# The looks at the weights' range placed in the idle stretches of ScalarE, with a third load buffer (HGRN2 attention followed by a multiplicative feed-forward block, one core)

## The chip, the cores and the metric

The kernel runs on one core of a Trainium2 chip. The metric is the device time of one execution in microseconds (us), the median over several runs.

## The reference

The input is a gated linear attention (4 batches, 8 heads, 768 steps, head size 48) whose output, joined over the heads to 3072 tokens of 384 numbers, goes through a feed-forward block with two parallel up projections that are multiplied.

```python
f = 1.0 / (1.0 + np.exp(-f_logit))
for t in range(S):
    state = f[:, :, t, :, None] * state + np.einsum('bhd,bhe->bhde', k[:, :, t], v[:, :, t])
    y[:, :, t] = np.einsum('bhd,bhde->bhe', q[:, :, t], state)
x = np.ascontiguousarray(y.transpose(0, 2, 1, 3)).reshape(B * S, H * D)
a = x @ w1          # 384 x 1024
b = x @ w2          # 384 x 1024
h = a * b @ w3      # 1024 x 1024
out = h @ w_out     # 1024 x 384
```

The q, k, v and f_logit arrays are float32. The four weight matrices are double precision in memory and are read as pairs of 32-bit words. The product of `w3` and `w_out` is formed once on the chip ("folding").

## The kernel before

**Two stages.** The attention goes through 24 chunks of 128 steps (`front`, `turning`, `rest`), in the first 260 us or so. The feed-forward block goes through six blocks of 512 tokens (`ffn(n)`), beside the attention as far as its inputs are there. Blocks 1 and 2 compute the up projections with seven products in the place of eight (`seven`, its matrix products are recorded at L959). Blocks 3 to 5 use a longer scheme of the same kind (`many`), whose products stand at L1114: each is two matmuls of 128x128 by 256 columns into one PSUM bank, `bank()`. The down projection is `down(i)`, at L863, two for each block, each with seven groups of four matmuls.

**What follows a product of `many`.** Several products are added up in one bank, one behind the other in a chain (`CHAINS`). Wherever a partial sum is needed by itself, ScalarE copies the bank into a temporary (`keep_`, L1135), and the next product of the chain may write the bank only after that copy. VectorE adds temporaries and banks (L1158), multiplies halves into the input of the down projection (L1170, L1177), and forms sums of inputs (L1081) and, for `down`, of `ab` (L1224). The end of `down` is at L1231 and L1244 on ScalarE (copies of banks), and at L1237, L1250, L1261, L1267 and L1275 on VectorE; its results leave by the stores at L1280.

**PSUM.** Beside four tiles of one bank each, named `f`, the two tiles `pa` and `py` of the attention have two banks each. Once the attention is done, their four halves join the pool "f", so that a product may go to either half of `pa` or `py`.

**The looks.** The fast path is right only if the weights lie in a certain range. `ranges()` reads the high word of every double again: 34 pieces of 128x1024 words, `load(i)` at L1513 by the DMA queue of SyncE, then two looks by ScalarE, `total(i)` at L1517 (sum of absolute values) and `count(i)` at L1521 (count of values over a bound), each with an accumulator. The pieces alternate between two buffers, the halves of the tile `A` (`both`). `verdict`, `judge`, `told`, `heard` and `decided` turn the sums into one number, `left`, over memory and back. It is read by all engines at L1272 behind the last down projection, and a branch follows it (L240).

**The order of the work** is written by a planner (`Plan`). Every piece of work is a task with an engine, a cost, tasks that it depends on and a priority. `order()` takes again and again the task that can start first on the planner's clock, and among equals the one with the lowest `prio`. The tasks are then emitted in this order, and each engine executes its own tasks in that order. A task may hold a slot of a pool: "f" is the PSUM banks and "t" the temporaries of `many` (11 of them, six beside the homes; numbers 4 and 5 lie in the tile `place`, columns 12864 to 13887). `temporary(i)` says where each lies.

In the kernel before, a look is a task like the others with a priority above all others in number (500 + i), so it is taken when ScalarE would else wait on the planner's clock. The planner knows PSUM by single banks. What the program waits for is worked out later, from the tiles that the instructions read and write.

Of the kernel before, what the change touches and what calls it, by code (L numbers as in the profile page):

```python
# [36 lines left out]
F32 = mybir.dt.float32  # L37
I32 = mybir.dt.int32
U32 = mybir.dt.uint32
# [16 lines left out]
TB = 512  # L56
# [14 lines left out]
WIDE = 2 * HP * C  # L71
LOOK = WIDE // 2
# [7 lines left out]
SURE_W = 2.0  # L80
# [5 lines left out]
HEAVY = 3  # L86
WITH_POOL = 0.6
LOOKS = 0.0
QLATE = 0.1
MANY = 3  # L90
W_LATE = 30
# [31 lines left out]
class Plan:  # L123
# [13 lines left out]

        self.pools[name] = [None] * n

    def add(self, eng, cost, emit, deps=(), prio=0.0, takes=(), frees=(), lag=0.2, slack=0.0, since=0.0, shared=False):  # L140


        t = {
            "eng": eng, "cost": cost, "emit": emit, "deps": [d for d in deps if d is not None], "prio": prio,
            "takes": list(takes), "frees": list(frees), "lag": lag, "slack": slack, "since": since, "shared": shared, "at": None, "end": None, "no": len(self.tasks),
        }
        self.tasks.append(t)
        return t

    def order(self):  # L150
        free, done, left = dict.fromkeys(("PE", "DVE", "ACT", "POOL", "SP"), BEGIN), [], list(self.tasks)
        enders, masking = {}, []
        for t in self.tasks:
            for f in t["frees"]:
                enders.setdefault(id(f), []).append(t)

        def after(t, ds):

            if any(d["end"] is None for d in ds):
                return None  # L160
            return max([0.0] + [d["end"] + (d["lag"] + t["slack"] if d["eng"] != t["eng"] else 0.0) for d in ds])

        def places(t, name):

            ends = [(after(t, enders[id(h)]) if h else 0.0, i) for i, h in enumerate(self.pools[name])]
            return [e for e in ends if e[0] is not None]

        def start(t):

            waits, at = list(t["deps"]), max(free.get(t["eng"], 0.0), t["since"])  # L170
            for name in t["takes"]:
                if name in self.pools:
                    ends = places(t, name)
                    if not ends:
                        return None
                    at = max(at, min(ends)[0])
                    continue
                n, taken = self.slots[name]
                if len(taken) >= n:
                    waits += enders[id(taken[-n])]  # L180
            ready = after(t, waits)
            if ready is None:
                return None
            at = max(at, ready)
            if t["shared"]:
                at += WITH_POOL * sum(max(0.0, min(at + t["cost"], b) - max(at, a)) for a, b in masking[-2:])
            return at

        def rank(t):

            return t["deps"][0]["end"] - 1e6 if t["eng"] == "DMA" else t["prio"]

        def slower(t, at):

            big = t["cost"] > 0.7
            return max([1.0] + [by[big] for a, b, by in CROWDED if a <= at < b]) if t["eng"] == "DMA" else 1.0

        while left:
            at, _, _, t = min(
                ((at, rank(t), t["no"], t) for t in left if (at := start(t)) is not None), key=lambda x: x[:3]  # L200
            )
            t["at"], t["end"] = at, at + t["cost"] * slower(t, at)
            free[t["eng"]] = t["end"]
            if t["eng"] == "POOL" and t["cost"] > 1.0:
                masking.append((t["at"], t["end"]))
            for name in t["takes"]:
                if name in self.pools:
                    t["got"] = min(places(t, name))[1]
                    self.pools[name][t["got"]] = t
                else:  # L210
                    self.slots[name][1].append(t)
            left.remove(t)
            done.append(t)
        return sorted(done, key=lambda t: (t["at"], t["no"]))
# [46 lines left out]
def ranged(ctx, tc, q, k, f_logit, v, w1, w2, w3, w_out, out, ident, w12, wc, left):  # L261
# [39 lines left out]
    def at(a, *shape):  # L301
        n = 1
        for m in shape:
            n *= m
        t = place[:, a : a + n]
        return t.rearrange("p (a b) -> p a b", a=shape[0]) if len(shape) == 2 else t
# [21 lines left out]
    def home(i):  # L328

        if i not in found:  # L330
            found[i] = homes[i]()
        return found[i]

    plan = Plan()
    plan.pool("f", NF)
    plan.pool("t", len(homes) - NWT + 6)
    plan.slot("a", 1)
    plan.slot("lane", 8)
    plan.slot("heavy", HEAVY)
# [13 lines left out]
    def temporary(i):  # L353

        if i < 2:
            return firsts[i]
        if i < 4:
            return ups[("u2", "u3")[i - 2]]
        return at(12864 + TB * (i - 4), TB) if i < 6 else home(NWT + i - 6)

    def idle(n):

# [67 lines left out]
    def moves(n, size, rate, emit, deps, prio, late=0.0, since=0.0, lanes=("lane",)):  # L430


        for j in range(n):
            i = plan.add("SP", 0.45, (lambda: None) if j else emit, [d] if j else deps, prio - j * 1e-3, takes=lanes, lag=0.85, since=since)
            d = i
            t = plan.add("DMA", size / n / rate, lambda: None, [i], prio - j * 1e-3, lag=1.1 + late, frees=[i])
        return t
# [1063 lines left out]
    def ranges():  # L1501

        seen = [w[kc * P : kc * P + P] for w in (w1, w2) for kc in range(KM)] + [w3[jc] for jc in range(KF)]
        seen.append(w_out.rearrange("(p a) c -> p (a c)", a=KF))
        seen = [w[:, c : c + LOOK] for w in seen for c in range(0, w.shape[1], LOOK)]
        n = len(seen)
        sums_, counts, small = (spare[:, a : a + m] for a, m in ((0, n), (64, n), (128, 1)))
        words = both.bitcast(U32)
        hi = words.rearrange("p (n two) -> p n two", two=2)[:, :, 1].bitcast(F32)
        last = [plan.add("DVE", 0.1, lambda: nc.vector.memset(small, -SMALL), [tk[NU - 1][nm] for nm in ("r", "v", "mid")] + [tk[NU - 2]["v"]], -20)]  # L1510

        def load(i):
            return lambda: nc.sync.dma_start(words[:, i % 2 * WIDE : (i % 2 + 1) * WIDE], seen[i].bitcast(U32))  # L1513

        def total(i):
            a = hi[:, i % 2 * LOOK : (i % 2 + 1) * LOOK]
            return lambda: nc.scalar.activation(a, a, AF.Abs, accum_out=sums_[:, i : i + 1])  # L1517

        def count(i):
            a = hi[:, i % 2 * LOOK : (i % 2 + 1) * LOOK]  # L1520
            return lambda: nc.scalar.activation(a, a, AF.Sign, bias=small, accum_out=counts[:, i : i + 1])  # L1521

        for i in range(n):
            ld = moves(1, LOOK, 400, load(i), last[:1] if i < 2 else last[i - 1 : i], 500 + i, SURE_W, since=LOOKS)
            a = plan.add("ACT", 0.92, total(i), [ld], 500 + i)
            last.append(plan.add("ACT", 0.95, count(i), [a], 500 + i))

        def verdict():
            nc.vector.tensor_scalar(sums_, sums_, LARGE, None, ALU.is_le)
            nc.vector.tensor_scalar(counts, counts, LOOK - 0.5, None, ALU.is_ge)  # L1530
            nc.vector.tensor_tensor(sums_, sums_, counts, ALU.mult)
            where["weights"] = small
            nc.vector.tensor_reduce(out=small, in_=sums_, axis=AX.X, op=ALU.min)

        return plan.add("DVE", 0.5, verdict, last, -20)
# [32 lines left out]
    for u in range(NU):  # L1568
        if u <= SOLO:
            front(u)  # L1570
        if NPE <= u <= SOLO:
            turning(u)
            begin(u)
        if u >= SOLO and u + 1 < NU:
            front(u + 1)
            turning(u + 1)
        rest(u)
        if u == 0:
            weights()
        if u == 3:  # L1580
            folding()
        if u == NU - 1:
            late = plan.add("none", 0.0, lambda: None)
            plan.pools["f"] += [late] * 4
            for nm in ("y", "mid", "m", "v"):
                tk[u][nm]["frees"].append(late)
            over["deps"] += [tk[u][nm] for nm in ("z", "v", "mid", "k", "q", "y")] + [tk[u - 1]["z"]]
            weighed = [ranges()] if wide else []
            looked = plan.add("DVE", 1.0, judge, [tk[i]["y"] for i in range(NU)] + weighed, -20)
            sent = moves(1, 0.4, 250, told, [looked], 0, 20.0)  # L1590
            judged = plan.add("DVE", 0.2, decided, [moves(1, 0.4, 250, heard, [sent], 0, 20.0)], -20)
        if u % UB == UB - 1:
            ffn(u // UB)
    first, last = {}, {}
# [396 lines left out]
```

## Time and profile before

| what | value |
|---|---|
| median of 3 runs | 466.19 us (465.18 to 466.82) |
| the profiled execution's own time | 466.62 us |
| its span, from the first to the last instruction | 464.9 us |
| TensorE matmul, busy | 454.4 us, 98% |
| VectorE, busy | 364.9 us, 78% |
| ScalarE, busy | 206.8 us, 44% |
| GpSimd, busy | 64.6 us, 14% |
| looks at L1517 | 34, mean 685 ns, first at 261.2 us, last at 401.3 us |
| looks at L1521 | 34, mean 781 ns, last at 402.5 us |
| loads of looks, L1513 | 34, 512 KB each, 3.4 to 5.1 us from issue to landing |

A share of the span is an average over stages. TensorE is the only engine near its full span; an idle stretch of another engine costs something only where TensorE has to wait for what that engine delivers. The profile gives one line to a group of equal instructions: source line, engine, operation, result and operands by the names of their tiles, shapes and count, busy time in us, mean of one in ns, and the idle time of the engine ahead of them with what ended it. Line numbers are those of the kernel before. In the changed kernel the same lines stand 31 further down from L150 on.

### The profile page before, as it was taken

Reading aid. Unit: us, or ns where it says so; the run is one execution under the profiler, and the core shown is the slowest. Engines: PE = TensorE matmul, PEld = TensorE weight load, DVE = VectorE, ACT = ScalarE, POOL = GpSimd, SP = SyncE. Lnnn points to the kernel's source line nnn. Section 1 sums busy time; section 2 is a strip of 40 time slices with the busy share of each in tenths; the row PEclk is TensorE's granted clock in tenths of the full one; section 3 lists DMA queues with packets and bytes.
Section 4 is the critical chain, followed back from the end, with each engine's and each line's share of the span. In section 5 each row is a group of like instructions: output and inputs, shape, how many; then the busy total and the mean of one; then the engine's idle time right before and its main releaser. Section 6 shows DMA issues by size and latency. Waiting matters only on the chain.

```text
span 464.9 us, 11763 instructions
## 1 busy us (share of the span) xinstructions
PE 454.4 (98%) x4800; PEld 396.0 (85%) x4800; DVE 364.9 (78%) x657; ACT 206.8 (44%) x468; POOL 64.6 (14%) x90
## 2 busy tenths in 40 slices
PE   8989999999999999999999999999999999999995
PEld 7778886666899888889998889998899977889995
DVE  8988999999898998989973599894687366867451
ACT  4565344532224444443332456565764567642000
POOL 9330001121122332322331000000000000000000
PEclk9999999999999999999999999999999999999999
DMA  6899898733346664545423336534364433100111
GB/s 180 263 307 282 276 347 276 261 96 93 83 111 191 200 181 122 140 134 165 106 64 107 120 124 204 170 129 151 119 202 159 151 122 94 45 1 0 35 68 39
DMA packets 43165, 68.75 MB, mean 148 GB/s; under 512 B 5201, under 2 KB 28242, under 8 KB 42082
## 3 DMA queue, kind: packets, MB, share of 16 engines
q1 hardware_dynamic: 43106, 67.95, 47.5%
q8 instruction: 39, 0.64, 0.6%
q14 instruction: 20, 0.16, 0.1%
HBM read 58.88 MB, written 9.04 MB: 146 GB/s over the span
## 4 chain that ended last, share of the span: by engine, by line
PE 94%; POOL 2%; DVE 1%; issue 1%; ACT 0%; POOLq 0%; DVEq 0%
PE f L863 25%; PE f L959 14%; PE f L1114 12%; PE f L1446 9%; PE pa L1114 5%; PE py L1114 5%; PE py L863 5%; PE pa L863 3%; PE py L619 3%; PE pa L545 2%; PE pa L652 2%; PE f L559 2%; PE py L638 2%; PE pa L959 1%; POOL ab L403 1%; PE f L365 1%
## 5 line engine op out<-in xcount | busy, mean ns | idle before, releaser
L675 POOL TENSOR_SCALAR_AFFINE_SELECT A<-A 64x512 f32<-64x512 f32 (+1 forms) x46 | 43.4, 943 | 104.5 <-ACT A L669 102.3
L1446 PE MATMUL f<-place 128*128 128x384 f32 x128 | 42.7, 488 | 0.0
L863 PE MATMUL f<-xt,w 128*128 128x256 f32 x192 | 42.1, 380 | 0.0
L863 PEld LDWEIGHTS f<-xt,w 128*128 128x128 f32 x192 | 36.3, 190 | 5.0
L1446 PEld LDWEIGHTS f<-place 128*128 128x128 f32 x128 | 23.8, 190 | 15.3
L959 PE MATMUL f<-xt,w 128*128 128x256 f32 x132 | 34.2, 379 | 0.0
L863 PE MATMUL f<-place 128*128 128x192 f32 x184 | 33.9, 329 | 0.0
L514 DVE TENSOR_TENSOR_SCAN bwd<-gate,back 112x512 f32<-112x512 f32 x24 | 30.9, 1285 | 0.7
L492 DVE TENSOR_TENSOR_SCAN fwd<-gate,floor 112x512 f32<-112x512 f32 x24 | 30.5, 1271 | 1.1 <-ACT gate L484 0.2
L863 PEld LDWEIGHTS f<-place 128*128 128x128 f32 x184 | 30.1, 190 | 0.8 <-DVE place L1237 0.3
L959 PEld LDWEIGHTS f<-xt,w 128*128 128x128 f32 x132 | 24.8, 190 | 3.1
L1521 ACT ACTIVATE A<-A,back 128x512 f32<-128x512 f32 x34 | 26.6, 781 | 0.5
L811 ACT ACTIVATE ys<-py 112x512 f32<-112x512 f32 x22 | 13.1, 595 | 28.2 <-PE py L638 27.3
L1384 ACT ACTIVATE place<-place 128x512 f32<-128x512 uint32 (+2 forms) x24 | 21.1, 890 | 9.9 <-DMA place<-in_w_dram 7.6
L1517 ACT ACTIVATE A<-A 128x512 f32<-128x512 f32 x34 | 23.3, 685 | 4.0 <-DMA A<-in_w_dram 4.0
L863 PE MATMUL f<-wc,ab 128*128 128x192 f32 x128 | 23.4, 326 | 0.0
L959 PE MATMUL f<-place 128*128 128x256 f32 x84 | 22.4, 385 | 0.0
L775 POOL TENSOR_TENSOR G<-lasts,gate 112x4 f32<-112x4 f32 x20 | 10.7, 533 | 81.3 <-ACT lasts L497 50.0
L863 PEld LDWEIGHTS f<-wc,ab 128*128 128x128 f32 x128 | 21.3, 190 | 0.3
L484 ACT ACTIVATE gate<-f 112x512 f32<-112x512 f32 x22 | 13.9, 632 | 15.8 <-DMA f<-in_f_logit_dram 5.6
L619 PEld LDWEIGHTS py<-A,vt 64*64 64x64 f32 (+1 forms) x672 | 13.3, 127 | 7.3 <-issue 5.7
L619 PE MATMUL py<-A,vt 64*64 64x64 f32 (+1 forms) x672 | 18.1, 223 | 0.2
(343 smaller groups left out, 1041.5 us busy)
## 6 DMA issues: line engine op xcount, KB each, us to landing
A<-in_w_dram SPq DMA_DIRECT2D x28, 512.0 KB, 3.9
place<-in_w_dram SPq DMA_DIRECT2D x8, 1024.0 KB, 6.7
place<-in_w_dram SPq DMA_DIRECT2D x12, 512.0 KB, 7.5
out_dram<-o SPq DMA_DIRECT2D x24, 192.0 KB, 1.9
q<-in_q_dram SPq DMA_DIRECT2D x46, 96.0 KB, 2.9
vt<-in_v_dram SPq DMA_DIRECT2D x23, 192.0 KB, 3.2
k<-in_k_dram SPq DMA_DIRECT2D x44, 96.0 KB, 2.6
yt<-ys SPq DMA_DIRECT2D x44, 96.0 KB, 2.7
```

Of the source, the lines that this page charges most:

```text
L484: nc.scalar.activation(gate[u % 2][:, 0:NQ], fu, AF.Sigmoid)
L492: nc.vector.tensor_tensor_scan(s["P"], gate[u % 2][:, 0:NQ], floor, 0.0, ALU.mult, ALU.max)
L514: nc.vector.tensor_tensor_scan(s["R"][:, ::-1], gate[u % 2][:, NQ:0:-1], back[:, ::-1], 0.0, ALU.mult, ALU.max)
L619: done = nc.tensor.matmul(y_block(u, hp, par, half)[p0 : p0 + w], lhsT=s["v"][half * W : half * W + W, h * D : h * D + w], rhs=s["A"][half ...
L675: nc.gpsimd.affine_select(out=a, in_=a, pattern=pattern, compare_op=ALU.is_ge, fill=0.0, base=0, channel_multiplier=-1,)
L863: nc.tensor.matmul(out_, lhsT=lhs[i], rhs=rhs[i], start=start and i == 0, stop=i == len(lhs) - 1, skip_group_check=True,)
L959: nc.tensor.matmul(q[nm][:, which * TH : which * TH + TH], lhsT=lhs[i](which), rhs=rhs[i], start=start and which == 0 and i == 0, stop=i = ...
L1114: nc.tensor.matmul(banks[g, c][:, which * TH : which * TH + TH], lhsT=lhs, rhs=x_node(a), start=first and which == 0, stop=True, skip_grou ...
L1384: nc.scalar.activation(lo.bitcast(F32), lo, AF.Copy, bias=2.0, scale=2.0**-51)
L1446: nc.tensor.matmul(w3s["p", jc], lhsT=w3s[jc][:, kc * P : kc * P + P], rhs=wos[:, kc], start=(kc == 0), stop=(kc == KF - 1),)
L1517: return lambda: nc.scalar.activation(a, a, AF.Abs, accum_out=sums_[:, i : i + 1])
L1521: return lambda: nc.scalar.activation(a, a, AF.Sign, bias=small, accum_out=counts[:, i : i + 1])
```

## The change

The looks leave the ordinary planning. `add` takes a list `gap`, and `order()` becomes two passes over the planner `listed()` (the old `order`). The first pass plans all work with the looks as tasks of no engine and no cost. From this plan it takes the idle stretches of ScalarE over `GAP` (0.2) long and puts each look, in turn, into the first stretch that holds its cost and `GAP`, not ahead of `FILL_FROM` (262) on the planner's clock, and not sooner than `RELOAD` (6.0) after the end of the look three pieces earlier that used its buffer. The second pass plans everything with each look bound to start no sooner than that place and with priority ahead of most other tasks.

The pieces go round three buffers: the two halves of `A` and columns 12864 to 13887 of `place`. The pool of temporaries has two less, 9 for 11. The first three loads also depend on the last product `m3` of every seven of block 1, since the third buffer holds inputs of that block. `SPREAD` (10.0) takes the place of 20.0 as the allowance for each of the two transfers of the verdict.

```diff
+GAP = 0.2
+FILL_FROM = 262.0
+RELOAD = 6.0
+SPREAD = 10.0
...
     def order(self):
+
+        fill = [t for t in self.tasks if t["gap"] is not None]
+        if fill:
+            was = [(t["eng"], t["cost"]) for t in fill]
+            for t in fill:
+                t["eng"], t["cost"] = "none", 0.0
+            slots, pools = ({n: (c, list(x)) for n, (c, x) in self.slots.items()}, {n: list(x) for n, x in self.pools.items()})
+            busy = sorted((t["at"], t["end"]) for t in self.listed() if t["eng"] == "ACT" and t["cost"])
...
+            for t, (t["eng"], t["cost"]) in zip(fill, was):
+                pass
+            gaps = [[a[1], b[0]] for a, b in zip(busy, busy[1:] + [(1e9, 1e9)]) if b[0] - a[1] > GAP]
+            at = {}
+            for t in fill:
+                low = max([FILL_FROM] + [at[g] + w for g, w in t["gap"] if g in at])
+                for g in gaps:
+                    a = max(g[0], low)
+                    if g[1] - a >= t["cost"] + GAP:
+                        break
+                t["since"], at[t["no"]], g[0] = a, a + t["cost"], a + t["cost"]
+        return self.listed()
+
+    def listed(self):
...
-    plan.pool("t", len(homes) - NWT + 6)
+    plan.pool("t", len(homes) - NWT + 4)
...
-        return at(12864 + TB * (i - 4), TB) if i < 6 else home(NWT + i - 6)
+        return home(NWT + i - 4)
...
-        words = both.bitcast(U32)
-        hi = words.rearrange("p (n two) -> p n two", two=2)[:, :, 1].bitcast(F32)
+        words = [t.bitcast(U32) for t in (*flat, at(12864, WIDE))]
+        his = [t.rearrange("p (n two) -> p n two", two=2)[:, :, 1].bitcast(F32) for t in words]
...
         for i in range(n):
-            ld = moves(1, LOOK, 400, load(i), last[:1] if i < 2 else last[i - 1 : i], 500 + i, SURE_W, since=LOOKS)
-            a = plan.add("ACT", 0.92, total(i), [ld], 500 + i)
-            last.append(plan.add("ACT", 0.95, count(i), [a], 500 + i))
+            ld = moves(1, LOOK, 400, load(i), last[:1] + [q["m3"] for q in blk[1]["seven"]] if i < 3 else last[i - 2 : i - 1], 500 + i, SURE_W, since=LOOKS)
+            a = plan.add("ACT", 0.92, total(i), [ld], -400 + i, gap=[(last[-1]["no"], 0.0)] + ([(last[i - 2]["no"], RELOAD)] if i > 2 else []))
+            last.append(plan.add("ACT", 0.95, count(i), [a], -400 + i, gap=[(a["no"], 0.0)]))
...
-            sent = moves(1, 0.4, 250, told, [looked], 0, 20.0)
-            judged = plan.add("DVE", 0.2, decided, [moves(1, 0.4, 250, heard, [sent], 0, 20.0)], -20)
+            sent = moves(1, 0.4, 250, told, [looked], 0, SPREAD)
+            judged = plan.add("DVE", 0.2, decided, [moves(1, 0.4, 250, heard, [sent], 0, SPREAD)], -20)
```

More of the change, by code (lines that the diff above doesn't have):

```diff
@@ L138, in pool, with add @@
         self.pools[name] = [None] * n
-    def add(self, eng, cost, emit, deps=(), prio=0.0, takes=(), frees=(), lag=0.2, slack=0.0, since=0.0, shared=False):
+    def add(self, eng, cost, emit, deps=(), prio=0.0, takes=(), frees=(), lag=0.2, slack=0.0, since=0.0, shared=False, gap=None):
         t = {
             "eng": eng, "cost": cost, "emit": emit, "deps": [d for d in deps if d is not None], "prio": prio,
-            "takes": list(takes), "frees": list(frees), "lag": lag, "slack": slack, "since": since, "shared": shared, "at": None, "end": None, "no": len(self.tasks),
+            "takes": list(takes), "frees": list(frees), "lag": lag, "slack": slack, "since": since, "shared": shared, "at": None, "end": None, "no": len(self.tasks), "gap": gap,
         }
@@ L150, in order @@
     def order(self):
+        fill = [t for t in self.tasks if t["gap"] is not None]
[5 more added lines that the diff above has]
+            busy = sorted((t["at"], t["end"]) for t in self.listed() if t["eng"] == "ACT" and t["cost"])
+            for t in self.tasks:
+                t["at"] = t["end"] = None
+                t.pop("got", None)
+            self.slots = {n: [c, x] for n, (c, x) in slots.items()}
+            self.pools = pools
+            for t, (t["eng"], t["cost"]) in zip(fill, was):
[11 more added lines that the diff above has]
+    def listed(self):
         free, done, left = dict.fromkeys(("PE", "DVE", "ACT", "POOL", "SP"), BEGIN), [], list(self.tasks)
@@ L1507, in ranges @@
         sums_, counts, small = (spare[:, a : a + m] for a, m in ((0, n), (64, n), (128, 1)))
-        words = both.bitcast(U32)
-        hi = words.rearrange("p (n two) -> p n two", two=2)[:, :, 1].bitcast(F32)
+        words = [t.bitcast(U32) for t in (*flat, at(12864, WIDE))]
+        his = [t.rearrange("p (n two) -> p n two", two=2)[:, :, 1].bitcast(F32) for t in words]
         last = [plan.add("DVE", 0.1, lambda: nc.vector.memset(small, -SMALL), [tk[NU - 1][nm] for nm in ("r", "v", "mid")] + [tk[NU - 2]["v"]], -20)]
         def load(i):
-            return lambda: nc.sync.dma_start(words[:, i % 2 * WIDE : (i % 2 + 1) * WIDE], seen[i].bitcast(U32))
+            return lambda: nc.sync.dma_start(words[i % 3], seen[i].bitcast(U32))
         def total(i):
-            a = hi[:, i % 2 * LOOK : (i % 2 + 1) * LOOK]
+            a = his[i % 3]
             return lambda: nc.scalar.activation(a, a, AF.Abs, accum_out=sums_[:, i : i + 1])
         def count(i):
-            a = hi[:, i % 2 * LOOK : (i % 2 + 1) * LOOK]
+            a = his[i % 3]
             return lambda: nc.scalar.activation(a, a, AF.Sign, bias=small, accum_out=counts[:, i : i + 1])
         for i in range(n):
-            ld = moves(1, LOOK, 400, load(i), last[:1] if i < 2 else last[i - 1 : i], 500 + i, SURE_W, since=LOOKS)
-            a = plan.add("ACT", 0.92, total(i), [ld], 500 + i)
-            last.append(plan.add("ACT", 0.95, count(i), [a], 500 + i))
+            ld = moves(1, LOOK, 400, load(i), last[:1] + [q["m3"] for q in blk[1]["seven"]] if i < 3 else last[i - 2 : i - 1], 500 + i, SURE_W, since=LOOKS)
+            a = plan.add("ACT", 0.92, total(i), [ld], -400 + i, gap=[(last[-1]["no"], 0.0)] + ([(last[i - 2]["no"], RELOAD)] if i > 2 else []))
+            last.append(plan.add("ACT", 0.95, count(i), [a], -400 + i, gap=[(a["no"], 0.0)]))
         def verdict():
```

## The prediction

> **What bounds the kernel now.** I read the page's busy times and its chain of waits first, then the busy time by 20 us stretches, then TensorE's waits, and last the timeline at each of them. All times below are of the profiled execution.
>
> ```profile
> PE 454.4 (98%) x4800; PEld 396.0 (85%) x4800; DVE 364.9 (78%) x657; ACT 206.8 (44%) x468; POOL 64.6 (14%) x90
> PE 94%; POOL 2%; DVE 1%; issue 1%; ACT 0%; POOLq 0%; DVEq 0%
> ```
>
> TensorE is busy 98% of the span and makes up 94% of the chain; ScalarE, on which the looks run, has 0% of it. So the change can only bring what TensorE loses, in the stretch where the order changes. The columns are the stretch, its length, then busy time and count of PE, PEld, DVE, ACT, POOL:
>
> ```profile
> 300.00:320.00 20.00, 20.00 (x108) 18.61 (x107) 16.03 (x36) 13.23 (x33) 0.00 (x0) 1.00 0.42 140
> 360.00:380.00 20.00, 19.07 (x97) 17.04 (x96) 8.64 (x17) 12.55 (x31) 0.00 (x0) 1.00 0.43 137
> 380.00:400.00 20.00, 19.32 (x89) 16.55 (x88) 14.15 (x25) 13.89 (x31) 0.00 (x0) 1.00 0.34 107
> 400.00:420.00 20.00, 20.00 (x93) 17.31 (x92) 15.63 (x39) 9.91 (x19) 0.00 (x0) 1.00 0.01 1
> ```
>
> From 260 us on TensorE has only two visible gaps, and ScalarE is half idle. TensorE's waits name them, and the timeline shows them, with two smaller ones (start, length, then what):
>
> ```profile
> PE pa L1114 <- ACT ys L1135: 0.9, 1, 0.9
> PE py L1114 <- ACT Q L1135: 0.7, 1, 0.7
> 358.03 1.46 PE L863 MATMUL pa<-wc,ab 128*128 128x192 f32 x8
> 359.46 1.57 PE L863 MATMUL f<-place 128*128 128x192 f32 x8
> 372.54 1.03 PE L1114 MATMUL f<-place,k 128*128 128x256 f32 x4
> 374.50 1.13 PE L1114 MATMUL pa<-xt,q 128*128 128x256 f32 x4 [0.93 <-ACT ys L1135]
> 383.23 1.03 PE L1114 MATMUL py<-xt,w 128*128 128x256 f32 x4
> 384.94 1.13 PE L1114 MATMUL py<-xt,w 128*128 128x256 f32 x4 [0.68 <-ACT Q L1135]
> 402.39 1.03 PE L1114 MATMUL f<-xt,k 128*128 128x256 f32 x4
> 403.38 1.13 PE L1114 MATMUL py<-place,floor 128*128 128x256 f32 x4
> ```
>
> Products that nothing holds start 0.865 us apart (372.54 less the product before it; the eight records of an L863 group 1.30). The record of 374.50 should therefore start at 373.40: 1.10 late, and it is 0.10 longer than its neighbours (1.13 for 1.03), 1.20 in all. In the same way 384.94 costs 0.84 + 0.10, 359.46 costs 0.13 + 0.11, 403.38 costs 0.13 + 0.10. Two more starts, at 334.46 and 387.93, are 0.08 late. **Sum after 260 us: 2.8 us.** That is the ceiling of any gain.
>
> What held them? ScalarE at the two large ones:
>
> ```profile
> 372.74 0.58 ACT L1135 COPY Q<-pa 128x512 f32<-128x512 f32 x1 [1.14 <-PE pa L1114]
> 373.22 0.66 ACT L1517 ACTIVATE A<-A 128x512 f32<-128x512 f32 x1
> 373.87 0.57 ACT L1135 COPY ys<-pa 128x512 f32<-128x512 f32 x1
> 384.30 0.59 ACT L1135 COPY Q<-py 128x512 f32<-128x512 f32 x1 [2.20 <-PE py L1114]
> ```
>
> At 373 a look of 0.65 us stands between two copies; TensorE waits for the second. But at 384 there is no look: ScalarE is idle for 2.2 us. A product into one half of `py` at 381.51 was followed by one into the other half at 383.23. The copy of the first half began only 0.2 after the *second* had ended (383.23 + 0.865 + 0.2 = 384.30), and the next product, into the other half again, waited for that copy of the first. At 373 the copy `Q<-pa` is held by the neighbouring half in the same way. In the program these copies and products do carry waits for the other half of the tile, which the planner, counting single banks, leaves out. So of 2.8 us the looks own about 0.65; the rest is **pairs of halves** of `pa` and `py`, and small delays of VectorE.
>
> **The Trainium skill.** "Perfetto Trace Analysis", section Optimization Strategy, says to find the gaps on the most contended engine and the semaphore behind each; that is the reading above. Its section Matmuls says that independent groups should rotate through PSUM banks so that the emptying of one overlaps the next. The trace agrees for the single-bank tiles `f` and disagrees for `pa` and `py`, where two banks are waited for as one (384.30). "DMA: Bandwidth & Descriptors", section Anatomy of one DMA, gives 2.0 us + bytes / 436 GB/s, by which 512 KB take 3.2 us, an estimate for another issue path; here the loads of looks take 3.4 to 5.1, and the trace's values are used.
>
> **The change, part by part.** I compared the order of both programs, engine by engine.
>
> *The looks.* 34 pairs before and after, each 0.79 + 0.86 us from start to start (359.74, 360.53, then free at 361.40): 56 us of ScalarE, moved and not removed. Up to 260 us TensorE's order is unchanged. In the new order, where a look stands ahead of a copy that TensorE needs at one product's distance, the copy before it belongs to a product two earlier (1.73), which holds its 0.48 and the look's 0.79 to 0.86: gain 0.65. The last look now stands directly behind the last L1174 copy but three downs, ahead of the L1231 copy. Those copies are at 428.74 and 433.09 before: free from 429.1, two looks end at 430.8. Nothing is pushed.
>
> *The third buffer.* A load may now be asked for while two others are unused. With two buffers ScalarE waited 4.0 us for loads (4 times, longest 2.2), none of it in TensorE's chain. SyncE's queue holds the loads ahead of stores and gathers in the same sequence as before, so nothing new stands behind a waiting load. Value 0; bounds: a gain of 0 and a loss of 2.2 less the 0.9 by which most copies lead their product, 1.3.
>
> *Two temporaries less.* A copy may wait for one VectorE sum more (0.69). TensorE's waits in the program at those places leave a product or more. Value 0, bounds 0 to 0.7.
>
> *SPREAD and the late verdict.* The thirteen small instructions of verdict and judge took 1.8 us (403.97 to 405.76) and now stand behind the L1224 of the fourth last down. Before, VectorE was free there from 431.39 to 432.65, so the L1267 behind them starts 0.55 late; the L1275 at 433.95 doesn't, and the product that follows that bank comes 3.9 us later. Hidden. `told` took 7.2 us to land: 433.2 + 7.2 = 440.4. `heard` stands behind four stores, the last one ready at 443.4; with as much again it lands at 450.6, and `decided` stands behind the L1261 of 457.35. Slack 6.7 us. Then `left` is there at 458.2, VectorE's own read of it (0.54) puts the last L1267 0.2 late and leaves the last L1275 (459.95, waiting for TensorE) where it is; SyncE's read (0.76) ends at 459.0, ahead of the last store. Value 0, bounds 0 to 0.3.
>
> *The new order of products.* This decides. From some 290 us on TensorE, ScalarE and VectorE are reordered. I looked in the new program for every product that waits for a copy or a sum, and counted the work between the product that this copy waits for and the waiting one. A copy needs 0.2 + 0.58 + 0.06 = 0.84 from its product's end (372.54 to 372.74; then 374.44 to 374.50). The same count on the kernel before gives 0.2 + 0.48 + 0.65 + 0.58 + 0.06 - 0.86 = 1.11 at 374.50 (seen: 1.10), 0.84 at 384.94 (seen: 0.84) and about 0.0 at two other places (seen: 0.08 each). In the new order:
> - One place like 374.50, without a look: two products into `pa`'s halves, one into `py`, then `pa` again, behind two copies: 0.2 + 0.48 + 0.58 + 0.06 - 0.86 = 0.46, + 0.10 = 0.56.
> - Four places with a distance of one product, about 0.08 each: 0.32.
> - No place like 384.94.
> - One group of L863 that waits for an L1177 behind two L1224 in VectorE's queue. If VectorE has no backlog it is just in time; with one sum of backlog 0.5. The nearest row is 403.38, 0.23 with restart; I take 0.3.
> - A sum on `pa` or `py` held by the other half now occurs at other places in VectorE's queue; 359.46 is what such a one cost (0.24). I take 0.1, bounds 0 to 0.5.
>
> Sum after: 0.56 + 0.32 + 0.3 + 0.1 = 1.3. **Difference: 2.8 - 1.3 = 1.5 us faster.** The profiled execution would go from 466.62 to 465.1. It stands 0.43 above the median, so against the median: 466.19 - 1.5 = 464.7.
>
> **Rivals.**
> - *As forecast*, 464.7, own range 464.0 to 465.4.
> - *The stalls come back.* VectorE's delays (both bounds, 0.5 + 0.5) and a temporary that is missed (0.7) add up: 1.3 + 1.3 = 2.6, nothing gained, 466.0. For it: VectorE is 80% busy in 300 to 320 us and 78% in 400 to 420. Against: it is 43% busy in 360 to 380.
> - *All stalls go:* 466.19 - 2.8 = 463.4. Against: the place of 0.56.
> - *Slower: pairs of halves in chains.* The new order is made by a planner blind to them. Each place like 384.94 that I have missed in 300 to 420 us costs 0.94. With 1.3 counted, the change is slower by over 1.4 us from a sum of 4.2, three more places; four give 466.19 - 1.5 + 3.8 = 468.5. Against: the same count found both large ones before.
> - *It doesn't do what it says:* the idle stretches are the planner's, and a copy held by a pair comes 0.86 late, into the look's place. That puts back 0.65: 465.3, inside the forecast.
>
> **How the numbers follow.** 0.3%, about what a measurement of this kernel can tell from no change, is 1.4 us: 464.8. The forecast has 0.62, of which six in ten lie below 464.8; stalls come back 0.18 (no change); all go 0.10 (faster); slower 0.10. Faster: 0.38 + 0.10 = 0.48; same 0.24 + 0.18 = 0.42; slower 0.10. The range goes from the ceiling, 463.4, to the forecast with the loss bounds of a load and of a temporary, 464.7 + 1.3 + 0.7 = 466.7; it takes in the case of no gain and leaves out the slower one.
>
> **What would show it.** TensorE's waits after 260 us: one for an L1135 copy of about 0.4 us near 338 us (four products behind the one of 334.46), none of 0.7 or more; the waits at 374 and 385 gone; 20 us stretches of 360 to 400 us at 19.8 or more. Looks spread to about 431 us, ScalarE's wait for loads under 4.0. It would be wrong if waits for copies of `pa` or `py` sum to over 1.5 us, if a product waits behind a look, or if the end between the last product and the end of the span grows beyond 5.4 us.

## The result and the profile after

| | before | after |
|---|---|---|
| median | 466.14 us (465.18 to 468.94, 22 runs) | 464.72 us (463.95 to 466.25, 22 runs) |
| the profiled execution's own time | 466.62 us | 464.53 us |
| its span | 464.9 us | 462.8 us |

The ratio is 0.997, 95% interval 0.9961 to 0.998: faster by 1.4 us, with a third of that as the uncertainty to either side. The forecast was 464.7 us.

The page after, first the busy times and then the chain of waits, hardly moves:

```profile
PE 454.1 (98%) x4800; PEld 395.6 (85%) x4800; DVE 364.8 (79%) x657; ACT 208.2 (45%) x468; POOL 64.7 (14%) x90
PE 93%; POOL 2%; DVE 2%; issue 1%; ACT 0%; POOLq 0%; DVEq 0%
```

All work is still there (4800 matmul records, 468 instructions of ScalarE); shares of the span cannot show 1.5 us. The 20 us stretches can (stretch, length, then PE, PEld, DVE, ACT, POOL busy):

```profile
320.00:340.00 20.00, 19.70 (x91) 16.63 (x90) 12.24 (x22) 10.66 (x22) 0.00 (x0) 1.00 0.21 73
360.00:380.00 20.00, 20.00 (x100) 18.01 (x99) 9.62 (x19) 12.15 (x27) 0.00 (x0) 1.00 0.43 143
380.00:400.00 20.00, 20.00 (x94) 17.44 (x93) 16.15 (x29) 13.41 (x29) 0.00 (x0) 1.00 0.29 88
420.00:440.00 20.00, 19.94 (x119) 19.33 (x118) 13.31 (x37) 6.04 (x15) 0.00 (x0) 1.00 0.08 21
```

360 to 380 and 380 to 400 were at 19.07 and 19.32 and are full; the loss now stands in 320 to 340. TensorE's waits name one copy after 260 us where there were two of 0.9 and 0.7:

```profile
PE pa L1145 <- ACT ys L1166: 0.3, 1, 0.3
```

The timeline there shows a place like the old one at 374.50, without a look:

```profile
335.86 1.03 PE L1145 MATMUL pa<-xt,w 128*128 128x256 f32 x4
336.72 1.03 PE L1145 MATMUL py<-xt,w 128*128 128x256 f32 x4
336.92 0.59 ACT L1166 COPY place<-pa 128x512 f32<-128x512 f32 x1 [1.32 <-PE pa L1145]
337.41 0.59 ACT L1166 COPY ys<-pa 128x512 f32<-128x512 f32 x1
338.05 1.13 PE L1145 MATMUL pa<-xt,K 128*128 128x256 f32 x4 [0.30 <-ACT ys L1166]
```

The copy `place<-pa` had to wait for the product of 335.86 into the other half of `pa` (end 336.72, plus 0.2), though its own half was ready a product earlier; the second copy starts 0.49 later, and the product of 338.05 waits for that one. Due at 337.59 (336.72 + 0.865), it is 0.46 late and 0.10 longer. The next largest is at 427.92:

```profile
426.12 0.68 DVE L1255 TENSOR_TENSOR place<-ab 128x512 f32<-128x512 f32 x1
426.83 0.69 DVE L1255 TENSOR_TENSOR place<-place,ab 128x512 f32<-128x512 f32 x1
427.45 0.42 DVE L1208 TENSOR_TENSOR ab<-pa,ab 128x256 f32<-128x256 f32 x1
427.92 1.57 PE L894 MATMUL pa<-wc,ab 128*128 128x192 f32 x8
```

The L1208 (before: L1177) stands behind two L1255 (before: L1224) in VectorE's queue without idle time, and the group into `pa` starts 0.22 late.

Counted by TensorE's starts, the stalls after 260 us are 0.46 + 0.10 (338.05), 0.22 + 0.10 (427.92), 0.07 + 0.10 (306.64), and 0.08 each at 323.03, 335.21 and 382.55: **1.29 us, where before had 2.76.** (The three of 0.08 are the second records of groups that started on time, at 322.74 for the first; so are 334.46 and 387.93 in the prediction.)

To see where time goes in a kernel whose order changes only late, compare the start of the same record of TensorE. Record 3600 starts at 247.78 us before; up to there TensorE's order is the same. The difference arises in the first 85 us and then stands still (in a_nolook alone, 0.46 of it comes later). From record 3600 to the last one is the stretch that the change touches. The last three columns of the table are read from the one profiled execution of each kernel. The medians are of 4 to 22 runs, and the ratios are to runs of the kernel before taken in the same series (median 465.88 to 466.26).

| kernel | median us | ratio to before, 95% | to record 3600, against before | from there to the last record, against before | last record to end of span |
|---|---|---|---|---|---|
| before | 466.14 | | 0 | 0 (211.80) | 5.30 |
| after | 464.72 | 0.9961 to 0.998 | -0.36 | -1.46 | 5.04 |
| b_nolook | 464.93 | 0.9965 to 0.9985 | +0.15 | -0.77 | 4.82 |
| a_nolook | 464.18 | 0.995 to 0.9977 | -0.18 | -1.47 | 5.13 |
| b_aware | 462.79 | 0.9917 to 0.9944 | -0.51 | -2.45 | 5.08 |
| b_aware_p2 | 463.75 | 0.9926 to 0.9965 | -0.53 | -2.46 | 5.19 |
| a_aware | 464.43 | 0.9953 to 0.9978 | -0.08 | -1.47 | 4.84 |
| b_pair2 | 467.81 | 1.0035 to 1.007 | -0.14 | +2.04 | 4.83 |
| a_pair2 | 472.41 | 1.0114 to 1.0147 | +0.40 | +6.11 | 5.06 |
| b_three | 468.88 | 1.0055 to 1.0117 | -0.98 | +3.43 | 4.94 |
| a_two | 474.82 | 1.0171 to 1.0202 | -0.53 | -1.36 | 15.70 |

Of the 2.1 us by which the spans differ, 1.46 is the changed stretch (and 2.76 - 1.29 = 1.47 the stalls), 0.36 the start, 0.26 the end.

### The profile page after: what moved, and what is told of

It is laid out like the page before. It is cut to its first block, busy times and chain, and to the rows that moved or that the text cites. A ratio compares the mean times of both kernels' runs of the same rounds, so it can differ in the third digit from the quotient of the medians.

```text
span 462.8 us, 11767 instructions
## 1 busy us (share of the span) xinstructions
PE 454.1 (98%) x4800; PEld 395.6 (85%) x4800; DVE 364.8 (79%) x657; ACT 208.2 (45%) x468; POOL 64.7 (14%) x90
## 4 chain that ended last, share of the span: by engine, by line
PE 93%; POOL 2%; DVE 2%; issue 1%; ACT 0%; POOLq 0%; DVEq 0%
PE f L894 26%; PE f L990 14%; PE f L1145 10%; PE f L1477 9%; PE pa L1145 7%; PE py L1145 5%; PE py L894 3%; PE py L650 3%; PE pa L894 3%; PE pa L576 2%; PE pa L683 2%; PE f L590 2%; PE py L669 2%; PE pa L990 1%; POOL ab L434 1%; PE f L396 1%
## 5 line engine op out<-in xcount | busy, mean ns | idle before, releaser
L894 PE MATMUL f<-place 128*128 128x192 f32 x216 | 39.5, 328 | 0.0
L1477 PEld LDWEIGHTS f<-place 128*128 128x128 f32 x128 | 23.8, 190 | 15.3
L894 PEld LDWEIGHTS f<-place 128*128 128x128 f32 x216 | 35.4, 190 | 0.5 <-issue 0.2
L1415 ACT ACTIVATE place<-place 128x512 f32<-128x512 uint32 (+2 forms) x24 | 21.1, 890 | 10.1 <-DMA place<-in_w_dram 7.9
L1552 ACT ACTIVATE A<-A,back 128x512 f32<-128x512 f32 x23 | 17.9, 778 | 0.3
L990 PEld LDWEIGHTS f<-place 128*128 128x128 f32 x84 | 15.3, 190 | 2.2 <-ACT place L1031 0.2
```

Source lines behind the costliest of these rows:

```text
L894: nc.tensor.matmul(out_, lhsT=lhs[i], rhs=rhs[i], start=start and i == 0, stop=i == len(lhs) - 1, skip_group_check=True,)
L990: nc.tensor.matmul(q[nm][:, which * TH : which * TH + TH], lhsT=lhs[i](which), rhs=rhs[i], start=start and which == 0 and i == 0, stop=i = ...
L1415: nc.scalar.activation(lo.bitcast(F32), lo, AF.Copy, bias=2.0, scale=2.0**-51)
L1477: nc.tensor.matmul(w3s["p", jc], lhsT=w3s[jc][:, kc * P : kc * P + P], rhs=wos[:, kc], start=(kc == 0), stop=(kc == KF - 1),)
```

## The experiments

Theory P is the prediction's: halves of `pa` and `py` hold each other, and the change gains because its new order happens to make less of this; the looks own some 0.65. Theory L says that the looks do it, theory S that start and end do. "The walk" in the expectations is the prediction's count carried through the whole order: each instruction starts when its engine is free and what it waits for in the program has ended, with the trace's durations (0.43 for a 128x256 matmul, 0.48 from copy to copy) and 0.2 after TensorE. Its sums leave out the places of 0.08 and the restarts (the 0.10 by which a group is longer after a stall), unless an expectation says that they are in.

**The looks left out, order kept** (b_nolook and a_nolook, with `% 2` and `% 3` buffers).

```diff
-            return lambda: nc.scalar.activation(a, a, AF.Abs, accum_out=...)
+            return (lambda: nc.scalar.activation(a, a, AF.Abs, accum_out=...)) if i < 1 else (lambda: None)
...
+        sums_, counts = sums_[:, 0:1], counts[:, 0:1]
```

> The kernel before in its own order on every engine, with 33 of the 34 pairs of looks left out (the loads stay, the verdict reads the first pair's columns only). Theory P (pairs of halves of pa and py hold copies and products for each other; a look only adds its length where it stands between two such copies): the stall at 374.5 us shrinks from 1.10 to about 0.45, the one at 384.9 us stays at 0.84 although no look is left, the one at 403 us goes; together 1.0 us off, 465.1 us. Theory L (looks that push copies aside make the stalls, and the change gains because it takes them out of the way): all large stalls go, 2.5 us off, 463.6 us. Theory S (the difference between the kernels lies in the start and in the end and not in the stalls): no change, 466.1 us.

> The changed kernel in its own order on every engine, with 33 of the 34 pairs of looks left out (the loads stay, the verdict reads the first pair's columns only). Theory P: in the changed order no look stands where TensorE waits, so the same stalls remain, 0.46 at 338 us and 0.22 at 428 us, and the time stays at 464.7 us. Rival: looks still hold copies at 338 or 428 us, or delay them elsewhere: up to 1.3 us off, 463.4 us.

The timeline of b_nolook at the two old places:

```profile
373.42 0.59 ACT L1135 COPY ys<-pa 128x512 f32<-128x512 f32 x1
374.06 1.13 PE L1114 MATMUL pa<-xt,q 128*128 128x256 f32 x4 [0.30 <-ACT ys L1135]
383.92 0.59 ACT L1135 COPY Q<-py 128x512 f32<-128x512 f32 x1 [2.92 <-PE py L1114]
384.56 1.13 PE L1114 MATMUL py<-xt,w 128*128 128x256 f32 x4 [0.73 <-ACT Q L1135]
```

With no look left, 374.06 is still 0.46 late (1.10 with the look, so the look owned 0.64), and 384.56 is 0.89 late (0.84 with the looks): ScalarE had been idle for 2.92 us and waited for the other half of `py`. The small stall at 403 is gone (0.23), and two others are longer by 0.08 together. In all -0.77; 1.0 was expected. In a_nolook the stalls are those of the changed kernel one by one (0.46 and 0.22, sum 1.29), and the stretch is the same, -1.47: in the changed order no look costs TensorE anything. Theory L holds for 0.77 of the 2.76 us of before and for no more. Of what the change gains it is a larger share: without looks the two orders still differ by 0.70 (-0.77 and -1.47), so about half of the 1.46 us comes from looks that no longer stand in the way, and half from the new order.

**A planner that knows the pairs** (b_aware: the looks, two buffers and 11 temporaries of before).

```diff
-            return [e for e in ends if e[0] is not None]
+            return [(max(e[0], read.get(tile_of(name, e[1]), 0.0)), e[1]) for e in ends if e[0] is not None]
...
+        def paired(t):
+            ws = [tile_of("f", o.get("got", 0)) for o in t.get("wr", [])]
+            rs = [tile_of("f", o.get("got", 0)) for o in t.get("rd", [])]
+            return max([0.0] + [read.get(x, 0.0) for x in ws] + [written.get(x, 0.0) for x in rs])
...
-            at = max(at, ready)
+            at = max(at, ready, paired(t))
```

`wr` and `rd` name, for each product, copy and sum, the product that opened the bank it writes or reads; `read` and `written` keep the latest end for each two-bank tile.

> The kernel before, its looks planned as before, two buffers, 11 temporaries, with one thing added to the planner: a task that reads a half of pa or py waits for the last product into either half, and a product into a half waits for the last reader of either half, as the program will. Theory P: walking the resulting order with the durations of the trace leaves one stall of TensorE after 260 us, 0.21 us at about 305 us, 0.3 with the restart, in the place of 2.8: 2.5 us off, 463.7 us, which is more than the change brings. Theory L: the looks stand as before and push copies aside as before, so no gain, 466.1 us, or a loss. Theory S: 466.1 us.

> b_aware with the banks paired as in a_pair2 and b_pair2 (slots 4 and 6 in pa, 5 and 7 in py), and the planner told of that pairing. Theory P: once the pairs are planned for, the pairing does not matter: one stall of about 0.25 us near 302 us as in b_aware, where the same pairing without planning cost 1.9 us (b_pair2) and 6.3 us (a_pair2); from the product at 247.8 us to the last one 2.45 us shorter than before, and the time 462.8 us if the 0.8 us that b_aware gained outside of that stretch is systematic, 463.5 us if it was the luck of the start. Rival: this pairing is bad by itself: 465 us or more.

The one stall that is left, in b_aware's timeline:

```profile
301.69 0.59 ACT L1161 COPY Q<-pa 128x512 f32<-128x512 f32 x1 [1.05 <-DVE place L1185]
302.33 1.13 PE L1139 MATMUL pa<-place,floor 128*128 128x256 f32 x4
```

The product of 302.33 is 0.25 late, as it waits for that copy (L1161, before: L1135); and the copy waits for VectorE (L1185, before: L1158), not for a pair. The stretch is 2.45 us shorter than before, as expected, and 1.0 shorter than in the changed kernel; b_aware is **the fastest kernel of this study**, faster than both, and contains no part of the change.

b_aware_p2 was meant as the same with the other pairing (next experiment), but it is no second case. Told of that pairing, the planner hands out the banks so that the same products share a tile again, and the two kernels emit one and the same program; their traces have the same instructions on the same tiles in the same order. Its -2.46 repeats the measurement and says nothing on the pairing. It ran on another chip than the other experiments: 462.79 (6 runs) and 463.75 us (12 runs) for one program show how far medians can lie apart here without a cause in the kernel.

**Other pairs** (a_pair2 and b_pair2: nothing is moved on any engine, only the bank of a slot).

```diff
-            nm = ("pa", "py")[(plan.got - NF) // 2]
+            nm = ("pa", "py")[(plan.got - NF) % 2]
...
-            return found[nm][:, plan.got % 2]
+            return found[nm][:, (plan.got - NF) // 2]
```

> The changed kernel in its own order on every engine, looks and loads included; only the banks are paired in another way (slots 4 and 6 in pa, 5 and 7 in py, where they were 4 and 5, 6 and 7). No instruction is added, removed or moved. Theory P: the walk gives 13 stalls after 260 us, 7.0 us in the place of 0.7, about 8.2 with the restarts (1.1 at 283 us, 0.6 each at 285, 287, 335 and 431 us, 0.44 at 326, 339, 381, 384, 409 and 417 us): some 7 us slower than the changed kernel, 471.5 us, slower than the kernel before as well. Theory L, and any theory in which the pairs do not matter: as the changed kernel, 464.7 us.

> The kernel before in its own order on every engine, with the banks paired as in a_pair2 (slots 4 and 6 in pa, 5 and 7 in py). Theory P: the walk gives 8 stalls after 260 us, 4.0 us, 4.8 with restarts, in the place of 2.8: 2 us slower than before, 468.1 us. With this pairing the change would then cost about 4 us (a_pair2 took 472.4) where with the other it gains 1.4: what the change brings is set by which halves its order happens to put in one tile. Rival: the two-bank tile is a fixed cost of the changed order alone, or the looks decide: b_pair2 stays at 466.1 us.

TensorE's waits in a_pair2, some of those that the changed kernel does not have:

```profile
PE pa L894 <- DVE place L1255: 0.9, 1, 0.9
PE py L1145 <- ACT place L1166: 0.6, 2, 0.3
PE py L1145 <- ACT ys L1166: 0.6, 2, 0.3
PE pa L894 <- ACT place L1262: 0.4, 1, 0.4
```

Two of b_pair2's that the kernel before does not have:

```profile
PE pa L863 <- DVE place L1237: 1.0, 2, 0.5
PE pa L863 <- ACT place L1231: 0.4, 1, 0.4
```

The same instructions in the same order take 7.57 us more in the stretch (+6.11 against -1.46; 8.2 less 1.3 was expected), and the order of before takes 2.04 more (2 was expected). With this pairing the change **costs** 4.1 us in the stretch where with the other it gains 1.5. For these two orders the sign of the difference depends on which halves share a tile.

**Two buffers in the place of three, under the new placing** (a_two).

```diff
-    plan.pool("t", len(homes) - NWT + 4)
+    plan.pool("t", len(homes) - NWT + 6)
...
-        words = [t.bitcast(U32) for t in (*flat, at(12864, WIDE))]
+        words = [t.bitcast(U32) for t in flat]
...
-            ... gap=[(last[-1]["no"], 0.0)] + ([(last[i - 2]["no"], RELOAD)] if i > 2 else []))
+            ... gap=[(last[-1]["no"], 0.0)] + ([(last[i - 1]["no"], RELOAD)] if i > 1 else []))
```

> The changed kernel with two buffers for the loads and 11 temporaries as before; the looks still go to the idle stretches of a plan without them, RELOAD counted from the look two pieces earlier. My prediction put the third buffer at 0, bounds 0 to 1.3 us of loss without it: 464.7 to 466.0 us. The walk says otherwise: TensorE's stalls stay near 1.0 us (0.44 at 337, 0.28 at 426, 0.24 at 455), but two buffers put the last look at about 455 us in the place of 427, the verdict is told at 459 us, lands 8.8 us later by the changed kernel's trace, is heard again 2 to 9 us later, and TensorE, which has to read it behind the last down, ends at 470 to 477 us: 475 to 482 us in all, 2 to 3.5% slower than before. Theory L: the gaps are what counts, 464.7 us.

The end of a_two in the timeline:

```profile
452.94 0.77 ACT L1552 ACTIVATE A<-A,back 128x512 f32<-128x512 f32 x1
456.15 0.33 SPq L1586 DMA_DIRECT2D good<-good  x1
463.45 0.30 SPq L1590 DMA_DIRECT2D row<-good  x1
466.73 0.27 DVE L1595 TENSOR_REDUCE least<-row 1x1 f32<-1x128 f32 x1 [9.74 <-DMA row<-good]
467.84 0.36 DVE L1306 TENSOR_TENSOR o<-pa,place 128x192 f32<-128x192 f32 x1 [0.67 <-DVE left L1596]
```

TensorE's stretch is like that of the changed kernel, with 11 temporaries in the place of 9 (-1.36 and -1.46). But the last look starts at 452.94 us (427.7 after), and VectorE then sits idle for 9.74 us until `row` is there, with the last L1306 (before: L1275) behind it: the piece at the end grows from 5.0 to 15.7 us, and the median is 10.1 us above the changed kernel's. The time is just under the expected 475 to 482: the verdict was told at 456.15 and not at 459, its store took 7.3 us and not 8.8, and `heard` took 3.3 (463.45 to 466.73) where 2 to 9 were allowed. The prediction's bound of 1.3 us, taken from waits for loads, is refuted as a bound on what the third buffer matters. `RELOAD` stayed at 6.0; a shorter one was not tried, so 10.1 us is the price of two buffers under this placing (the kernel before, with two, starts its last look at 402.5 us).

**The third buffer alone** (b_three, planned as before).

```diff
-            a = plan.add("ACT", 0.92, total(i), [ld], -400 + i, gap=...)
+            a = plan.add("ACT", 0.92, total(i), [ld], 500 + i)
```

> One part of the change alone: the third buffer (with its 9 temporaries and its loads behind m3), the looks planned as before, SPREAD 20. Theory P: the looks come at other times on the planner's clock and the order changes with them; the walk gives 12 stalls after 260 us, 5.5 us, 6.7 with restarts, in the place of 2.8: 3.9 us slower than before, 470 us (1.06 at 376 us and 0.82 at 362 us behind VectorE, 0.83 at 425 and 0.61 each at 349 and 351 us on pairs of halves). Rival: the buffer by itself takes waits for loads away, or does nothing: 464.7 to 466.1 us.

TensorE's waits, three of those that are new:

```profile
PE py L1145 <- ACT place L1166: 1.0, 2, 0.7
PE pa L1145 <- DVE ab L1208: 0.9, 1, 0.9
PE py L894 <- DVE place L1281: 0.5, 1, 0.5
```

Measured +3.43 in the stretch, 6.2 us of stalls with restarts at the expected places (one of them half as long, 0.42 at 363.84), of which 0.84 at 427.62 and 0.61 each at 350.71 and 352.73 wait on `py`, and 1.04 at 378.02 for an L1208. The buffer by itself is another order, and a worse one.

**The change on top of the planner that knows the pairs** (a_aware, the edit of b_aware in the changed kernel).

> The changed kernel, with the planner that knows the pairs, as in b_aware. Theory P: the walk leaves two stalls, 0.71 at 431 us and 0.61 at 438 us, both behind VectorE just after the instructions of the verdict, which the planner books shorter than they are; 1.5 us with restarts, in the place of 0.3 in b_aware: 464 to 465 us, 1.2 us slower than b_aware. Then the change brings nothing of its own once the pairs are planned for, and its late verdict costs a little. Rival: the change still has a gain of its own (looks out of the way): at or below b_aware's 462.8 us.

The timeline of a_aware around the verdict, its first and last instruction among them, and at the second stall (L1310 and L1297 are L1250 and L1237 of the kernel before):

```profile
424.86 0.17 DVE L1590 TENSOR_SCALAR back<-back 128x34 f32<-128x34 f32 x1
426.51 0.16 DVE L1611 TENSOR_TENSOR good<-good,back 128x1 f32<-128x1 f32 x1
428.32 0.34 DVE L1310 TENSOR_TENSOR place<-py,place 128x192 f32<-128x192 f32 x1
428.72 1.57 PE L918 MATMUL py<-place,ab 128*128 128x192 f32 x8 [0.22 <-DVE place L1310]
435.58 0.36 DVE L1297 TENSOR_TENSOR place<-pa,place 128x192 f32<-128x192 f32 x1 [3.00 <-PE pa L918]
435.99 1.24 PE L918 MATMUL pa<-place 128*128 128x192 f32 x6 [0.51 <-DVE place L1297]
```

VectorE has no idle time from 424.86 to 428.32: 1.7 us of small instructions stand ahead of the L1310 that TensorE needs, and it loses 0.38 + 0.10 (0.71 was expected). The second stall, 0.67 + 0.10 at 435.99, came in size and nearly in place, but for another reason than I gave: VectorE had been idle for 3.00 us before its sum at 435.58, which waited for both groups into `pa`. So, by this reading, a late verdict costs 0.5 here, and the pairs are not wholly planned away. The stretch is at -1.47 against -2.45 for b_aware: with the pairs planned for, the change brings nothing here, and its order is 1.0 us worse.

## Why the prediction was right

- *What bounds the kernel:* right. What is gained is what TensorE no longer loses after 260 us, 1.46 us of a ceiling of 2.8.
- *The looks' own 0.65:* 0.64 at 374 (b_nolook), and none of it is left after (a_nolook). Missed: the stall at 403, which I had put down to VectorE alone, also goes without the looks, so that they owned 0.77 net.
- *Pairs of halves:* right, by b_nolook (0.89 without a look), by b_aware and by a_pair2. The walk put its sum for each order on record before the run, restarts in it: 0.3 for b_aware, 1.5 for a_aware, 4.8 for b_pair2, 6.7 for b_three, 8.2 for a_pair2. Measured were 0.35, 1.3, 4.8, 6.2 and 8.9, the places of 0.08 among them.
- *The new order,* term by term: the place near 338 us 0.56, measured 0.56; four places of 0.08, measured three; no place like 384.94, and none came; the L863 group behind two L1224 0.3, measured 0.32; the VectorE sum 0.1, measured 0.17 at 306.64. The sum of 1.3 was measured at 1.29. That it fits so closely is in part luck: 0.3 and 0.1 were taken from inside bounds of 0 to 0.5, and the place of 0.08 that did not come makes up for what they lacked. So is a median within 0.02 of the forecast, when the difference is uncertain by a third. The profiled execution was forecast at 465.1 and took 464.53, by the start and the end (0.36 + 0.26), which I had kept as they were. That these go with the change is not shown.
- *Two temporaries less,* 0: a_two, with 11, has the same stalls.
- *The third buffer,* 0: right for the sum (ScalarE waited 1.8 us for loads of looks, 4.0 before), **wrong as an account of the part**. I had bounded it by what ScalarE waits for loads, 0 to 1.3. What it does is to set when the last look can stand: under the new placing two buffers cost 10.1 us through the verdict. The step that failed is that I asked who waits for a load, and not when the last one is over.
- *SPREAD and the late verdict,* 0: right, with less room than it looks. `told` landed after 8.8 us (7.2 before), all engines read `left` at 456.3, and the last record of TensorE starts at 457.76. In a_aware the small instructions (twelve in the traces, not thirteen) do cost TensorE 0.48. `left` was there 1.9 us sooner than the 458.2 of the prediction.
- *Rivals.* "Slower by pairs of halves" did not occur, but its mechanism is what decides: with another pairing it gave 472.4 us, more than its 468.5. I had this as places that I might have missed in the order; it is rather a coincidence of order and pairing. "All stalls go", 463.4, took place in b_aware (0.35 left).

Open: the start differs by -0.98 to +0.40 us between kernels whose order is the same there, nearly all of it in the first 85 us. It is as large as half of the effect and more, and theory S is left with that: 0.62 us of one profiled execution. b_aware's median gained 3.3 us, 0.8 more than its stretch; none of the 1.0 us between it and b_aware_p2 belongs to the kernel, as that is the same program. Not run: four tiles of one bank each in the place of `pa` and `py` once the attention is done, which would take the pairs away altogether; and the third way to pair the four halves.

## What to carry to other kernels

Where a planner books banks and the program waits by tiles, each order is a draw: count the waits of the program that was built before crediting a change with its gain, and teach the planner what the program waits for, which here brought more (2.45 us) than moving the looks (1.46). Test a change of order with something that does not touch the order, such as another assignment of banks; if the sign turns, the gain belongs to the order and the assignment together, and not to the change by itself. Of a work that nobody waits for, ask when its last piece ends: two buffers for three moved no stall of TensorE's and, under this placing, cost 10 us at the end.

## What the runs showed of the hardware

The store of the verdict, 0.5 KB from 128 partitions, took 7.2 us (before), 8.8 us (after) and 7.3 us (a_two) from issue to landing, longer than the looks' loads of 512 KB (3.4 to 5.3 us after); the load back of the same 0.5 KB into one partition took 3.3 us in a_two, from issue to VectorE's first instruction on it. And the first record after nearly every longer stall of TensorE was 0.07 to 0.10 us longer, whatever the stall (0.07 at 306.64, 1.10 at 374.50) and the shape (256 or 192 columns). At the places of 0.08 the same shows without a stall: the group of 322.74 starts on time and lasts 1.11 us where its neighbours last 1.03.
